# Bias tables in fewer operations, turned keys in a bank of their own, due times moved: one attention and two expert layers on one core

## Chip, core and metric

One core of a Trainium2 chip runs the whole program once per execution. The metric is the device time of one execution in microseconds, the median of several runs. TensorE (PE) multiplies matrices and turns (transposes) tiles, VectorE (DVE), ScalarE (ACT) and GpSimd (POOL) work element by element, SyncE (SP) issues transfers.

## Reference

Three layers follow each other on two sequences of 768 tokens: windowed attention with 8 heads of 64, a gated expert layer, and an expert layer with a layer norm.

```python
scores = scale * q @ k.T                       # per head, 768 x 768
keep = (j < n_global) | ((i - j >= 0) & (i - j < n_local))      # n_global 8, n_local 96
dist = where(j < n_global and not local, n_local, abs(i - j))
scores = where(keep, scores - slope[h] * dist, -1e9)
a = softmax(scores);  x = a @ v
xk, xr = mu_k * x + (1 - mu_k) * x_prev, mu_r * x + (1 - mu_r) * x_prev
x = sigmoid(xr @ w_r) * (relu(xk @ w_k) ** 2 @ w_v)             # 512 -> 1024 -> 512
x = x + relu(layernorm(x) * g_ln @ w_ch1) @ w_ch2               # 512 -> 2048 -> 512
```

All arrays arrive as 8-byte numbers or 4-byte floats. The large weights are 8-byte and are put together into 4-byte words on the chip.

## The kernel before

**Attention.** The 1536 tokens are 12 blocks of 128 (6 for each sequence). A block `n` is done in two half-blocks `i = 2n` and `2n + 1` of four heads each, 24 in all, counted from 0. Block 0 and block 6 see 128 columns, the others 232 (the band and the global columns). For each block its queries and keys are loaded (`plan_loads`, L402 for queries, L353, L354, L356 for keys; L356 and L353 also carry the values), turned on TensorE (L443, in `plan_turn`), and copied to SBUF: queries by VectorE, which scales them (L450), keys by ScalarE (L343 into `b0h`). A half-block then goes through these steps: scores on TensorE (L496); bias added and minimum taken by VectorE (L509, once per head); exponent on ScalarE (L515, once per head); turning of the weights on TensorE into the PSUM tile `b45` (L546, four or eight instructions); one copy `yy<-b` of that tile to SBUF on ScalarE (L343); and the product with the values on TensorE (L561, written x8 in the order and x16 in the profile for a full half-block). There is one tile `b45`, so the weights of half-block `i + 1` can be turned only when the copy of half-block `i` is done. After a block, the inverse sums are spread out, turned on TensorE (L598 in `plan_out`) and multiplied in.

**PSUM banks.** Bank 3 takes the turned queries, the turned keys of all blocks but block 0, and the turned sums (L598). Bank 7 takes the turned keys of block 0, the warm-up products (L248), fillers (L527: products of the identity, of no use to the result, twelve pairs behind the scores of half-blocks 0 to 3), and later the products of the gate.

**Bias tables.** `constants()` makes the table `nb0` (128 x 128, for blocks 0 and 6) and `nb` (128 x 456, for all others) on VectorE from index ramps by GpSimd: L277 to L285 make `nb0`, L288 to L296 make `nb`. The two counts `n_global` and `n_local` arrive in the tile `words` by a transfer of ScalarE's queue (L61). `nb0` is written out before any planned operation, `nb` in four steps that the planner places.

**Weights and expert layers.** Each 512 x 128 piece of 8-byte weights is loaded into `stage` and put together by VectorE in three operations (L628, L629, L630) and split in two parts by ScalarE and GpSimd. The mix of neighbouring tokens (L699 on GpSimd, L704 on VectorE), the gate's products (L755), the hidden layer (L791), the output (L828 to L830), the norms (L871 turns them), and the last layer (L1089 up, L1190 to L1192 down) follow. The gate's products and the first hidden products may run between half-blocks of attention.

**What sets the order.** Every operation is registered with engine costs, the cells that it reads and writes, the buffers ("rooms") that it needs, and a due time. `Plan.play` then simulates a clock for each engine and writes the instructions out in the order in which it picks them: always the one with the smallest pair of earliest start and due time. So a due time decides only between operations that could start at the same moment, and each engine runs its instructions in the order written. `CLOCK` gives the times at which the engines are taken to be free first.

```python
key = (t, due, i, e)
if best is None or key < best:
```

SyncE issues transfers in order too, and a transfer that waits for a buffer holds up those behind it.

## Time and profile before

| | |
|---|---|
| median of 3 runs | 538.32 us (538.18 to 539.33) |
| the profiled execution's own time | 538.67 us |
| its span, first to last instruction | 536.9 us |
| granted TensorE clock | 0.999 of full speed |
| TensorE busy | 525.2 us (98%) |
| VectorE, ScalarE, GpSimd busy | 409.3, 297.7, 284.3 us |

The profiled execution took 1.8 us more than its span and 0.35 us more than the median. A busy share is the time in which an engine had an instruction in work. In the timeline a bracket behind a row is the time for which the engine sat idle before it, with the engine and line that ended it.

### The profile page before, as it was taken

To read this page: it belongs to the slowest core of one execution; us is meant where nothing else is said; L and a number is where in the kernel's file an instruction comes from. 1 tells how busy PE (TensorE), PEld (TensorE's weight loads), DVE (VectorE), ACT (ScalarE), POOL (GpSimd) and SP (SyncE) were. 2 spreads that over 40 slices of the span, in tenths; PEclk is the share of its full clock that TensorE was granted. 3 is DMA by queue.
4 is the path that set the end of the run, shared out by engine and by line. 5 is a ranking of instruction groups with operands and counts; after the bars stand their busy time and mean duration, and the time that the engine had idled before them with its cause. 6 is when DMAs were issued, how large, how long until landed. Compare 5 with 4: busy or idle time off the path is not lost.

```text
span 536.9 us, 8949 instructions
## 1 busy us (share of the span) xinstructions
PE 525.2 (98%) x3231; PEld 457.5 (85%) x3231; DVE 409.3 (76%) x819; ACT 297.7 (55%) x656; POOL 284.3 (53%) x348
## 2 busy tenths in 40 slices
PE   8989999999999999999999999999999999999996
PEld 6867677888899898989888898989888898989885
DVE  5789887973996537558999777687799887778554
ACT  3788979877453235374677453653555446365320
POOL 2387656774855022152249463784785758478300
PEclk9999999999999999999999999999999999999999
DMA  8994584320320000021122003113130321311024
GB/s 161 261 215 99 142 209 121 99 80 2 117 80 2 0 2 1 0 80 40 39 80 78 1 0 117 41 49 109 40 114 5 91 67 43 116 40 39 1 79 159
DMA packets 52110, 40.52 MB, mean 75 GB/s; under 512 B 40928, under 2 KB 41184, under 8 KB 52064
## 3 DMA queue, kind: packets, MB, share of 16 engines
q1 hardware_dynamic: 51200, 39.01, 26.3%
q10 hardware_dynamic: 864, 0.92, 0.5%
q8 instruction: 26, 0.43, 0.3%
q14 instruction: 20, 0.16, 0.1%
HBM read 36.77 MB, written 3.15 MB: 74 GB/s over the span
## 4 chain that ended last, share of the span: by engine, by line
PE 83%; DVE 11%; ACT 2%; DMA 1%; issue 1%; POOL 1%; ACTq 0%; DVEq 0%; SPq 0%
PE b L1089 20%; PE b L791 11%; PE b L1190 8%; PE b L1192 8%; PE b L1191 8%; PE b L755 6%; PE b L496 4%; PE b L561 4%; PE b L546 3%; PE b L828 3%; PE b L830 3%; PE b L829 3%; PE b L443 1%; PE b L527 1%; DVE stage L629 1%
## 5 line engine op out<-in xcount | busy, mean ns | idle before, releaser
L629 DVE SCALAR_TENSOR_TENSOR stage<-stage 128x512 int32<-128x512 int32 x50 | 49.1, 981 | 1.0
L630 DVE SCALAR_TENSOR_TENSOR cv<-cv,stage 128x512 int32<-128x512 int32 x50 | 44.6, 893 | 5.5 <-ACT cv L343 3.8
L515 ACT ACTIVATE t0l<-t0l,mn 128x232 f32<-128x232 f32 (+1 forms) x96 | 44.4, 466 | 6.9 <-DVE mn L509 6.8
L699 POOL TENSOR_SCALAR rt<-xg,vec 128x256 f32<-128x256 f32 x48 | 32.2, 685 | 17.6 <-DVE yy L806 8.8
L1206 DVE TENSOR_TENSOR xg<-b,xg 128x512 f32<-128x512 f32 (+1 forms) x51 | 33.9, 674 | 7.6 <-PE b L1192 6.3
L1108 POOL TENSOR_TENSOR h<-e,h 128x384 fp32r<-128x384 f32 x14 | 17.4, 1243 | 42.2 <-ACT h L343 41.8
L1108 POOL TENSOR_TENSOR h<-rt,h 128x384 fp32r<-128x384 f32 x28 | 37.3, 1331 | 1.7 <-ACT h L343 1.6
L1104 ACT ACTIVATE e<-e 128x384 f32<-128x384 f32 x16 | 8.4, 525 | 47.0 <-DVE e L1097 46.6
L509 DVE CUSTOM_DVE_ANT_0 t0l<-b,ln 128x232 f32<-128x232 f32 x80 | 27.6, 393 | 7.6 <-PE b L496 7.6
L640 POOL TENSOR_TENSOR s<-cv,s 128x384 fp32r<-128x384 f32 (+1 forms) x22 | 25.3, 1154 | 15.0 <-ACT s L636 14.9
L791 PE MATMUL b<-b0l,t1l 128*128 128x256 f32 x144 | 31.7, 281 | 0.0
L628 DVE TENSOR_SCALAR stage<-stage 128x512 int32<-128x512 int32 x50 | 31.0, 619 | 0.8 <-DMA stage<-in_moe_w_ch_dram 0.4
L1196 DVE TENSOR_TENSOR xg<-b,xg 128x1024 f32<-128x1024 f32 x23 | 28.0, 1217 | 4.6 <-PE b L1192 4.2
L704 DVE SCALAR_TENSOR_TENSOR rt<-xg,vec,rt 128x256 f32<-128x256 f32 x48 | 29.6, 662 | 0.6 <-POOL rt L699 0.6
L546 PE MATMUL b<-ident,t0l 128*128 128x128 f32 x176 | 28.8, 282 | 0.1
L1089 PE MATMUL b<-t0h,s 128*128 128x384 f32 x128 | 27.9, 339 | 0.0
L561 PE MATMUL b<-yy,h 128*64 128x128 f32 x352 | 24.5, 279 | 3.3 <-ACT yy L343 3.2
L1089 PE MATMUL b<-t1h,s 128*128 128x384 f32 x128 | 27.6, 337 | 0.0
L866 POOL TENSOR_SCALAR st<-st 128x1 f32<-128x1 f32 x12 | 3.1, 255 | 46.1 <-DVE st L863 45.8
L1033 ACT ACTIVATE cv<-cv,vec 128x256 f32<-128x256 f32 x32 | 14.5, 502 | 23.2 <-DVE cv L630 23.2
L343 ACT ACTIVATE yy<-b 128x1024 f32<-128x1024 f32 (+1 forms) x24 | 22.7, 945 | 7.7 <-PE b L546 7.5
L755 PE MATMUL b<-s,h 128*128 128x512 f32 x96 | 25.8, 404 | 0.0
(316 smaller groups left out, 1708.7 us busy)
## 6 DMA issues: line engine op xcount, KB each, us to landing
stage<-in_moe_w_ch_dram SPq DMA_DIRECT2D x26, 512.0 KB, 3.8
stage<-in_moe_w_k_dram SPq DMA_DIRECT2D x8, 512.0 KB, 4.8
stage<-in_moe_w_v_dram SPq DMA_DIRECT2D x8, 512.0 KB, 3.6
stage<-in_moe_w_ch_dram SPq DMA_DIRECT2D x12, 256.0 KB, 3.0
b0l<-in_q_dram SPq DMA_DIRECT2D x7, 256.0 KB, 3.3
h<-in_v_dram SPq DMA_DIRECT2D x6, 256.0 KB, 5.5
h<-in_v_dram SPq DMA_DIRECT2D x6, 192.0 KB, 4.0
stage<-in_moe_w_r_dram SPq DMA_DIRECT2D x2, 512.0 KB
```

Source lines behind the costliest of these rows:

```text
L515: nc.scalar.activation(t, t, AF.Exp, bias=mn.tile[:, k : k + 1], scale=-1.0, accum_out=sm.tile[:, h : h + 1])
L546: nc.tensor.transpose(b.tile[:, c, k * P : (k + 1) * P], tp.tile[:, o : o + P], self.ident)
L561: nc.tensor.matmul(o, V[c].tile[:, h * D : (h + 1) * D], y.tile[:, c, k * P : (k + 1) * P], start=c == 0, stop=c == m - 1)
L629: p.op({"DVE": 760}, lambda e: nc.vector.scalar_tensor_tensor(low(), high(), -(1 << 31), low(), ALU.bitwise_and, ALU.bitwise_or), [R, (R, ...
L630: p.op({"DVE": 760}, lambda e: nc.vector.scalar_tensor_tensor(y(), y(), 3, low(), ALU.logical_shift_left, ALU.bitwise_or), [(R, 2)], [C], ...
L755: nc.tensor.matmul(b.tile, *seq[s], start=s == 0, stop=s == 11)
L791: nc.tensor.matmul(o, l, r, start=s == 0, stop=s == 11)
L1089: nc.tensor.matmul(acc(x), lhs(i, c, n), rhs(r, j, c), start=y == 0, stop=y == 5)
L1108: lambda e: (nc.vector if e == "DVE" else nc.gpsimd).tensor_tensor(o(1), V(y), o(0).bitcast(F32), ALU.subtract),
L1190: nc.tensor.matmul(ps, hi, wh, start=f == 0, stop=False)
L1191: nc.tensor.matmul(ps, hi, wl, start=False, stop=False)
L1192: nc.tensor.matmul(ps, lo, wh, start=False, stop=f == 1)
```

## The change

1. The bias tables are made with maximum instead of masks: both tables in 13 VectorE operations in place of 15. `nb0` is now planned too, in two steps that wait for `words` (taken to arrive at 5.4 us) and are due 0.6 us after the first block's own due time.
2. The turned keys of blocks 0 to 5 go to bank 7; those of blocks 6 to 11 stay in bank 3.
3. The planner's first free times change (`CLOCK`: TensorE 5.2 to 5.5, VectorE 6.2 to 2.8), transfers start its clock at 2.4 us, and sizes of loads are counted smaller (keys, queries and values by 15%, weights by 37%).
4. Due times of some 20 kinds of operation move, from a fraction of a microsecond to 47 us.

```diff
-CLOCK = {"PE": 5.2, "ACT": 3.0, "DVE": 6.2, "POOL": 4.0, "SP": 0.8}
+CLOCK = {"PE": 5.5, "ACT": 3.0, "DVE": 2.8, "POOL": 4.0, "SP": 0.8, "WORDS": 0.0}
...
-        nc.vector.tensor_scalar(M[:, o], R[:, o], 0.0, None, ALU.is_ge)
+        nc.vector.tensor_scalar(M[:, o], R[:, o], 0.0, BIG, ALU.is_lt, ALU.mult)
+        nc.vector.tensor_tensor(R[:, o], R[:, o], M[:, o], ALU.max)
+        yield
         nc.vector.tensor_copy(f, self.words[:, :, 0])
-        nc.vector.tensor_scalar(G0, J, ng, None, ALU.is_lt)
-        nc.vector.scalar_tensor_tensor(L[:, o], R[:, o], nl, M[:, o], ALU.is_lt, ALU.mult)
-        nc.vector.tensor_tensor(M0, G0, L[:, o], ALU.max)
-        nc.vector.scalar_tensor_tensor(D0, R[:, o], nl, L[:, o], ALU.subtract, ALU.mult)
-        nc.vector.tensor_scalar(M0, M0, -BIG, BIG, ALU.mult, ALU.add)
-        nc.vector.tensor_scalar(D0, D0, nl, None, ALU.add)
-        nc.vector.tensor_tensor(self.nb0, D0, M0, ALU.add)
+        nc.vector.tensor_scalar(M[:, o], R[:, o], nl, BIG, ALU.is_ge, ALU.mult)
+        nc.vector.tensor_scalar(J, J, ng, BIG, ALU.is_ge, ALU.mult)
+        yield
+        nc.vector.tensor_tensor(nb[:, o], R[:, o], M[:, o], ALU.max)
+        nc.vector.scalar_tensor_tensor(self.nb0, J, nl, nb[:, o], ALU.add, ALU.min)
         yield
...
-            p.op({"SP": 60}, lambda e, h=h: nc.sync.dma_start(by_head(qr())[:, h], q[:, h]), (), self.sides(n, s, "q", n % 3), qrooms, due, size=size)
+            p.op({"SP": 60}, lambda e, h=h: nc.sync.dma_start(by_head(qr())[:, h], q[:, h]), (), self.sides(n, s, "q", n % 3), qrooms, due - 20, size=size)
...
-                b = self.bank_room(7 if n == 0 and x == "k" else 3)
+                b = self.bank_room(7 if n < 6 and x == "k" else 3)
...
-        p.op({"PE": 436}, turn, [("x", n)], [("R", n)], [X, b], due + 1)
+        p.op({"PE": 436}, turn, [("x", n)], [("R", n)], [X, b], due + 11)
...
-            p.op({"POOL": 1200}, first, xs + [("vec", 3)], [Y], [X, y] + rooms, due, behind=behind)
+            p.op({"POOL": 1200}, first, xs + [("vec", 3)], [Y], [X, y] + rooms, due - 10, behind=behind)
...
+            p.op({"WORDS": 5400}, lambda e: None, (), ["words"])
+            rooms = [self.token("rt", 2) for _ in range(2)]
+            for ns in (700, 600):
+                p.op({"DVE": ns}, lambda e: next(bias), ["words"], [("nb", False)], [*rooms, self.VW, self.bias], self.due(0) + 0.6)
```

On TensorE, ScalarE, GpSimd and SyncE the same work stands in another order, but for a few small copies and two conversions that go to another engine. The three places of which the rest speaks follow.

VectorE at the start of the program. Before; `words` holds the counts, `rt`, `h1` and `e` the tables in the making, L450 copies the first turned queries out of bank 3:

```order
L277 TENSOR_SCALAR rt_6_92<-rt_5_91 128x128
L278 CAST low_4_90<-words_65 128x2
L279 TENSOR_SCALAR h1_1_74<-h1_1_74,low_4_90 128x128
L280 SCALAR_TENSOR_TENSOR e_7_93<-rt_5_91,low_4_90,rt_6_92 128x128
L281 TENSOR_TENSOR h1_1_74<-h1_1_74,e_7_93 128x128
L282 SCALAR_TENSOR_TENSOR h1_1_74<-rt_5_91,low_4_90,e_7_93 128x128
L283 TENSOR_SCALAR h1_1_74<-h1_1_74 128x128
L284 TENSOR_SCALAR h1_1_74<-h1_1_74,low_4_90 128x128
L285 TENSOR_TENSOR h1_1_74<-h1_1_74 128x128
L450 TENSOR_TENSOR b0l_12_123<-b3_19_156,qs_9_111 128x256
```

And now:

```order
L277 TENSOR_SCALAR rt_6_92<-rt_5_91 128x128
L278 TENSOR_TENSOR rt_5_91<-rt_5_91,rt_6_92 128x128
L583 MEMSET xg_15_134 128x4
L583 MEMSET xg_16_136 128x4
L280 CAST low_4_90<-words_65 128x2
L281 TENSOR_SCALAR rt_6_92<-rt_5_91,low_4_90 128x128
L282 TENSOR_SCALAR h1_1_74<-h1_1_74,low_4_90 128x128
L450 TENSOR_TENSOR b0l_11_115<-b3_20_155,qs_8_103 128x256
L284 TENSOR_TENSOR ln_7_100<-rt_5_91,rt_6_92 128x128
L285 SCALAR_TENSOR_TENSOR h1_1_74<-h1_1_74,low_4_90,ln_7_100 128x128
L450 TENSOR_TENSOR b0l_11_115<-b3_21_161,qs_8_103 128x256
```

The first copy of queries stood behind all nine operations of `nb0`; now two of its operations and the second copy stand behind it.

SyncE's first transfers, before: queries go to `b0l` (those of block 2 to `b0h`), keys to `u`, and the shape 128x4x64 is half of block 0:

```order
L402 DMA b0l_12_123<-in_q_dram 128x4x64
L356 DMA u_13_125<-in_k_dram 128x4x64
L402 DMA b0l_12_123<-in_q_dram 128x4x64
L356 DMA u_13_125<-in_k_dram 128x4x64
L402 DMA b0l_12_123<-in_q_dram 128x8x64
L353 DMA u_13_125<-in_k_dram 96x8x64
L354 DMA u_13_125<-in_k_dram 32x8x64
```

And now:

```order
L402 DMA b0l_11_115<-in_q_dram 128x4x64 x2
L402 DMA b0l_11_115<-in_q_dram 128x8x64
L356 DMA u_12_119<-in_k_dram 128x4x64 x2
L402 DMA b0h_13_122<-in_q_dram 128x8x64
L353 DMA u_12_119<-in_k_dram 96x8x64
L354 DMA u_12_119<-in_k_dram 32x8x64
```

All queries of blocks 0 and 1 are now issued ahead of the first keys, and those of block 2 ahead of the keys of block 1.

TensorE around half-block 4 (the first half of block 2), whose weights are turned into `b45_77` in both programs. Before, from the values' product of half-block 3 on:

```order
L561 MATMUL b6_65_371<-yy_39_239,h1_1_74 64x128 x8
L546 MATMUL b45_77_445<-ident_60,t0l_18_153 128x128 x8
L561 MATMUL b6_82_472<-yy_39_239,h1_1_74 64x128 x8
L443 MATMUL b3_84_489<-ident_60,u_13_125 128x128 x4
L546 MATMUL b45_85_496<-ident_60,t0l_18_153 128x128 x8
L443 MATMUL b3_86_509<-ident_60,b0l_12_123 128x128 x4
L561 MATMUL b6_82_472<-yy_39_239,h1_1_74 64x128 x8
```

And now, from the same product on to the one of half-block 4:

```order
L561 MATMUL b6_70_400<-yy_39_256,h1_1_74 64x128 x8
L443 MATMUL b7_76_449<-ident_60,u_12_119 128x128 x4
L546 MATMUL b45_77_458<-ident_60,t0l_19_149 128x128 x8
L598 MATMUL b3_79_472<-ident_60,xg_15_134 128x128 x4
L496 MATMUL b0_80_479<-b0h_13_122,b0l_11_115 128x232
L496 MATMUL b1_81_480<-b0h_13_122,b0l_11_115 128x232
L496 MATMUL b0_80_479<-b0h_13_122,b0l_11_115 128x232
L496 MATMUL b1_81_480<-b0h_13_122,b0l_11_115 128x232
L443 MATMUL b3_82_488<-ident_60,b0l_11_115 128x128 x4
L443 MATMUL b7_84_495<-ident_60,u_12_119 128x128 x4
L561 MATMUL b6_87_507<-yy_39_256,h1_1_74 64x128 x8
```

Before, the product of half-block 4 (second L561) stands directly behind the turning of its weights; now the turning of sums, the scores of half-block 6 and two turnings of block 4 stand between them.

## Rows read from the trace of the kernel before

**Rows 1.** The page, part 1: TensorE's busy time and share of the span.
```profile
PE 525.2 (98%) x3231; PEld 457.5 (85%) x3231; DVE 409.3 (76%) x819; ACT 297.7 (55%) x656; POOL 284.3 (53%) x348
```

**Rows 2.** Waits of TensorE: engine line <- releaser: us in total, times, longest.
```profile
PE b L561 <- ACT yy L343: 3.2, 4, 1.2
PE b L1190 <- DVE xg L1196: 0.7, 1, 0.7
PE b L871 <- ACT ln L876: 0.6, 1, 0.6
PE b L598 <- DVE b0l L450: 0.4, 1, 0.4
```

**Rows 3.** Timeline of TensorE, 28 to 66 us; idle time before a row in brackets.
```profile
32.12 1.09 PE L561 MATMUL b<-yy,h 128*64 128x128 f32 x16 [1.17 <-ACT yy L343]
33.64 1.04 PE L546 MATMUL b<-ident,t0l 128*128 128x128 f32 x8
35.96 1.09 PE L561 MATMUL b<-yy,h 128*64 128x128 f32 x16 [0.77 <-ACT yy L343]
55.52 1.09 PE L561 MATMUL b<-yy,h 128*64 128x128 f32 x16 [0.41 <-ACT yy L343]
64.25 1.09 PE L561 MATMUL b<-yy,h 128*64 128x128 f32 x16 [0.82 <-ACT yy L343]
```

**Rows 4.** The chain that ended last, 27 to 43 us: start, us, what.
```profile
27.03 0.44 PE b L598 x4
27.46 0.98 PE b L496 x8
28.45 1.02 PE b L561 x16
41.36 1.39 PE b L755 x6
```

**Rows 5.** Timeline of ScalarE, 62 to 65 us: start, us, engine, line, what.
```profile
63.14 1.01 ACT L343 ACTIVATE yy<-b 128x1024 f32<-128x1024 f32 x1
64.04 0.60 ACT L343 ACTIVATE b0h<-b 128x512 f32<-128x512 f32 x1
64.52 0.49 ACT L515 ACTIVATE t0l<-t0l,mn 128x232 f32<-128x232 f32 x1
```

**Rows 6.** Windows, 43.00 to 59.96 us: length, then busy time of each engine.
```profile
43.00:59.96 16.96, 16.55 (x140) 12.57 (x138) 14.13 (x43) 14.90 (x41) 11.51 (x14) 1.00 0.50 125
```

**Rows 7.** Timeline of the first 8 us, VectorE, TensorE and the DMA queue.
```profile
0.84 0.43 SPq L402 DMA_DIRECT2D b0l<-in_q_dram  x1
2.96 0.50 SPq L402 DMA_DIRECT2D b0l<-in_q_dram  x1
5.29 0.17 DVE L278 CAST low<-words 128x2 f32<-128x2 int32 x1 [3.13 <-DMA words<-in_n_local_dram]
5.53 0.63 PE L443 MATMUL b<-ident,b0l 128*128 128x128 f32 x2
7.17 0.41 PE L443 MATMUL b<-ident,u 128*128 128x128 f32 x2 [0.51 <-ACT b0h L343]
7.28 0.42 DVE L450 TENSOR_TENSOR b0l<-b,qs 128x256 f32<-128x256 f32 x1
7.62 0.38 ACT L343 ACTIVATE b0h<-b 128x256 f32<-128x256 f32 x1 [0.29 <-PE b L443]
7.75 0.72 PE L496 MATMUL b<-b0h,b0l 64*128 64x128 f32 x8 [0.16 <-DVE b0l L450]
```

**Rows 8.** DMA issues at 0.84 and 2.96 us: KB, us to landing.
```profile
b0l<-in_q_dram SPq DMA_DIRECT2D x1, 128.0 KB, 3.1
b0l<-in_q_dram SPq DMA_DIRECT2D x1, 256.0 KB, 5.4
```

**Rows 9.** VectorE's rows on `stage`, 40 to 140 us: ns min/median/max.
```profile
L629 DVE SCALAR_TENSOR_TENSOR stage<-stage x14: 675/692/1655, 44.0 to 139.2; 128x512 int32<-128x512 int32 x14
```

**Rows 10.** Groups by line, 0 to 140 us: mean ns of one.
```profile
L704 DVE SCALAR_TENSOR_TENSOR rt<-xg,vec,rt 128x256 f32<-128x256 f32 x23 | 15.1, 696 | 0.0
```

More of the change, by code (lines that the diff above doesn't have):

```diff
@@ L256, in constants @@
         ng, nl = f[:, 0:1], f[:, 1:2]
-        y = [self.t([P, 512], x, bufs=2) for x in ("rt", "rt", "e")]
         C = 2 * WW - MAXG
-        R, M, L = (z[:, 0:C] for z in y)
-        self.nb0, J, G0 = (self.vw[:, 5 * 512 + i * P : 5 * 512 + (i + 1) * P] for i in range(3))
-        D0, M0 = J, G0
+        R, M = (self.t([P, 512], "rt", bufs=2)[:, 0:C] for _ in range(2))
+        self.nb0, J = (self.vw[:, 5 * 512 + i * P : 5 * 512 + (i + 1) * P] for i in range(2))
         iota = lambda x, pattern, base, m: nc.gpsimd.iota(
@@ L413, in plan_values @@
         due = self.due(2 * n) - 4
-        p.op({"SP": 60}, lambda e: self.att_rows(by_head(y.tile), v[t0 : t0 + P], n), (), [("v", n % 4)], [y], due, size=P * DM * 4)
+        p.op({"SP": 60}, lambda e: self.att_rows(by_head(y.tile), v[t0 : t0 + P], n), (), [("v", n % 4)], [y], due, size=P * DM * 3.4)
         g = lambda: self.VW.tile[:, 2048:2560]
@@ L584, in plan_out @@
             else:
-                p.op({"DVE": 170, "ACT": 300}, lambda e: self.copy(e, X.tile[:, :, 0:1], self.X[g - 1].tile[:, :, GT : GT + 1]), [("x", n - 1)], [("x0", g)], [X, self.X[g - 1]], due)
+                p.op({"DVE": 170, "ACT": 300}, lambda e: self.copy(e, X.tile[:, :, 0:1], self.X[g - 1].tile[:, :, GT : GT + 1]), [("x", n - 1)], [("x0", g)], [X, self.X[g - 1]], due + 6)
         sums = [("sm", n, h) for h in range(H)]
@@ L793, in plan_k @@
                     {"PE": 1440}, products, [("xk", g, s, i) for s in range(2) for i in range(2)] + [("m1", c + 4 * (f // 4)) for c in range(4)],
-                    [("kp", g, fp)], rooms + [b] + sorted({self.Wr[c + 4 * (f // 4)][0] for c in range(4)}, key=lambda x: x.tag), due + 3 * fp + 1.5 * u,
+                    [("kp", g, fp)], rooms + [b] + sorted({self.Wr[c + 4 * (f // 4)][0] for c in range(4)}, key=lambda x: x.tag), due + 3 * fp + 1.5 * u + 1.5,
                 )
@@ L835, in plan_v @@
                 [b[tb], *dict.fromkeys(self.k2[g][f // 2][0] for f in fs), *dict.fromkeys(self.Wr[12 + f][0] for f in fs)],
-                due + (3 * n if last else f0), behind=[self.last_pv],
+                due + (3 * n if last else f0) - 1.5, behind=[self.last_pv],
             )
@@ L884, in plan_norm @@
             else:
-                p.op({"ACT": 590}, lambda e: self.copy(e, hi(), chunks(b.tile)), [N], [("B", s, i, 0)], [b, X[0]], due + 3)
-            p.op({"DVE": 715} if early else {"POOL": 1440}, lambda e: sub(e, lo(), chunks(F()), hi().bitcast(F32)), [("F", j), ("B", s, i, 0)], [("B", s, i, 1)], [prep, *X[0:2]], low_due, behind=up)
+                p.op({"ACT": 590}, lambda e: self.copy(e, hi(), chunks(b.tile)), [N], [("B", s, i, 0)], [b, X[0]], due + 14.5)
+            p.op({"DVE": 715} if early else {"POOL": 1440}, lambda e: sub(e, lo(), chunks(F()), hi().bitcast(F32)), [("F", j), ("B", s, i, 0)], [("B", s, i, 1)], [prep, *X[0:2]], low_due + 21.5, behind=up)
             return
@@ L892, in plan_norm @@
         Tt = [("Tt", k) for k in range(4)]
[L893 to L895 removed]
+        p.op({"ACT": 590}, lambda e: self.copy(e, y.tile, b.tile), [], [N], [b, y], due + 3.7)
+        p.op({"DVE": 350}, lambda e: sub(e, T(0), y.tile[:, 0:256], F()[:, 0:256]), [N, ("F", j)], [Tt[0]], [y, prep], due - 16.2)
+        p.op({"DVE": 350}, lambda e: sub(e, T(1), y.tile[:, 256:512], T(0)), [N, Tt[0]], [Tt[1]], [y, prep], due)
         if late:
@@ L899, in plan_norm @@
             p.op({"ACT": 400}, lambda e: self.copy(e, keep(), y.tile[:, 256:512]), [N], [K], [y, prep], due + 3)
-            p.op({"ACT": 400}, lambda e: self.copy(e, hi(), pair(keep())), [K], [("B", s, i, 0)], [prep, X[2]], low_due, behind=[self.x_op])
+            p.op({"ACT": 400}, lambda e: self.copy(e, hi(), pair(keep())), [K], [("B", s, i, 0)], [prep, X[2]], low_due - 20, behind=[self.x_op])
             p.op({"POOL": 700}, lambda e: sub(e, lo(), pair(keep()), hi().bitcast(F32)), [K, ("B", s, i, 0)], [("B", s, i, 1)], [prep, *X[2:4]], low_due)
@@ L1108, in put @@
                 lambda e: (nc.vector if e == "DVE" else nc.gpsimd).tensor_tensor(o(1), V(y), o(0).bitcast(F32), ALU.subtract),
-                [("v", k, y), (*U, 0)], [(*U, 1)], [v[y], h], due + order[x] + 2,
+                [("v", k, y), (*U, 0)], [(*U, 1)], [v[y], h], due + order[x] - 18,
             )
         product("P1", 0, 0)
-        p.op({"ACT": 500}, lambda e: self.copy(e, V(11), acc("P1")), [("up", k, "P1")], [("v", k, 11)], [v[11], banks["P1"]], due + order["P1"] + 1)
+        p.op({"ACT": 500}, lambda e: self.copy(e, V(11), acc("P1")), [("up", k, "P1")], [("v", k, 11)], [v[11], banks["P1"]], due + order['P1'] + 47)
         product("P6", 4, 4)
@@ L1192, in go @@
                         nc.tensor.matmul(ps, lo, wh, start=False, stop=f == 1)
-                    p.op({"PE": 690 if c == whole else 360}, go, [("h", k, f, T, z) for z in range(2)] + [("w2", 2 * q + 1 - f)], [A], [h, rooms[i], chunks[f][0]], d + (0.1 if k else 1.5) * nth + 0.01 * f)
+                    p.op({"PE": 690 if c == whole else 360}, go, [("h", k, f, T, z) for z in range(2)] + [("w2", 2 * q + 1 - f)], [A], [h, rooms[i], chunks[f][0]], d + (0.1 if k else 1.5) * nth + 0.01 * f + 3)
                 cells.append(A)
```

62 lines of the change are left out of this document (30 added, 32 removed).

## Prediction

> **What bounds the kernel now.** Read first the busy shares: TensorE works in 98% of the span [rows 1]. The work on TensorE is the same in both programs, only its order differs, so a faster VectorE or a shorter table is worth nothing in itself: the time changes by what TensorE's idle time changes. The second view is therefore TensorE's own waits [rows 2]. After the first turned queries they come to about 5.6 us in all, and they are the whole stake: 3.2 us in four waits of the values' product (L561) for ScalarE's copy `yy` of the turned weights, 0.4 us of the turned sums (L598) for a copy out of bank 3, 1.3 us in two waits at the passage to the last layer (L871, L1190), and 0.7 us before the first scores [rows 7]. The timeline then shows where the four stand: 1.17 us at 32.12, 0.77 at 35.96, 0.41 at 55.52 and 0.82 at 64.25 [rows 3], which are half-blocks 4, 5, 8 and 10. These four and the one of L598 are all that attention has after its start [rows 2].
>
> Why there? Half-block 4 shows it in the order: the product stands directly behind the turning of its own weights. ScalarE needs 1.01 us for the copy [rows 5], TensorE has nothing in between, and it waits 1.17 us. In half-blocks 5 and 10 one turning of 0.44 us lies between, in 8 some 1.8 us did and still did not do, because ScalarE reached the copy late.
>
> **The start, and the tables.** Before, VectorE begins the nine operations of `nb0` when the counts are there (5.29 us) and takes the first turned queries out of bank 3 at 7.28, though they were turned by 6.16 (5.53 + 0.63) [rows 7]. In the new order only the cast and two operations stand ahead, done by about 6.2, so this copy starts about 1.1 us earlier. This does not make the first scores 1.1 us earlier, because they also need turned keys, and the keys are now the fourth transfer instead of the second. A transfer of 128 KB issued first, at 0.84, landed after 3.1 us, at 3.94; the fifth, with which 768 KB had been asked for, was issued at 2.96 and landed after 5.4, at 8.36 [rows 7, 8]. Between these two points lie 4.42 us for 640 KB. The first keys now complete 640 KB, so I estimate them at 3.94 + 512/640 x 4.42 = 7.5 us; before they completed 256 KB, 4.8 us, and nothing waited for them. The queries of block 2, which now have to be turned before the second scores, complete 1024 KB: 10.1 us. The keys of block 1, which the queries of block 2 now pass too, complete 1280 KB, 11.9 us; they are turned behind second scores, three fillers and the first weights, so after 12 us in any case.
>
> Walked through: second half of queries turned from 6.7 (0.5 idle before) to 7.1; 0.4 idle until the keys; keys turned to 7.9; the queries of block 1 turned while ScalarE copies the keys (0.38) [rows 7]; scores at about 8.4, where they were at 7.75; then the second keys, turned by 9.6, and 0.5 idle for the queries of block 2, behind which the second scores and all else on TensorE stand. That is 1.4 us idle against 0.7: **+0.7 us**. Later the early turnings need not be done again, so a later first score alone costs nothing. Bounds: if no transfer is late, only the first 0.5 is left (-0.2); if the first keys land where the fifth transfer did, at 8.4, +1.6.
>
> The rule that speaks against this edit is in the Trainium skill, "DMA: Bandwidth & Descriptors", section on queues, rings and completion order: each engine consumes a queue's descriptors in ring order, so queries put ahead of keys are served ahead of them. The two landings agree as far as they go. By the fabric ceiling of 435 GB/s among that page's specifications, the 384 KB put in front would cost an estimated 0.9 us, the keys would land at about 5.7, and the start would come out at -0.2 + 0.5 = +0.3 us; the rows show a slower queue.
>
> The six operations of the larger table are as many as before and lie between first scores and their use three half-blocks later, behind fillers: nothing. The shorter `nb0` by itself: nothing beyond the above.
>
> **Attention between 30 and 70 us.** The new order puts half-block i + 2's scores between the turning of half-block i and its product, everywhere from half-block 4 on. One such piece is scores of 0.98 and one turning of 0.44 to 0.48, so at least 1.4 us of cover where there was none or 0.44; half-block 4 has four pieces, 0.44 + 0.98 + 2 x 0.44 = 2.3 us [rows 4]. Waits plus cover were 1.17, 1.21 and 1.26 us for half-blocks 4, 5 and 10, so 1.4 us covers all three.
>
> Can ScalarE keep this pace? In half-blocks 5 to 9 a cycle of TensorE is one product (1.02), one turning of weights (1.04), scores (0.98) and one small turning (0.44): 3.48 us [rows 3, 4]. ScalarE has four exponents, the copy and one or two copies of a turned tile. From start to start the copy takes 0.90 and a small one 0.48 [rows 5]; with exponents at 0.48, the stretch between two copies, in which three exponents and two small copies stand, is 0.90 + 0.96 + 1.44 = 3.3 us. So it fits with 0.18 to spare, and a late exponent will still be felt now and then. I leave two waits of the size seen at half-block 8, 0.41 each: 0.8, and 0.1 for the rest. The 0.4 at L598 was a wait for queries' copy out of bank 3; with the keys gone from that bank it has two users for each block instead of three, and I count this wait as gone. **3.55 - 0.9 = -2.65 us.** Bounds: no wait left (-3.55); a wait of 0.41 in each of seven half-blocks (-0.7).
>
> **What moves without price.** The gate's products, moved out of half-blocks 6 to 9 to behind half-block 12, are done by TensorE in any case; they were cover there, and later they still are. If attention ends 2 us earlier, the next that could be late are the hidden layer's weight pieces, for which TensorE waits nowhere now; (b) below prices that. The operations moved in the hidden and last layers stand where TensorE does not idle, except the passage with 1.3 us. I change nothing there: between 0 and -1.3 if the new order also removes these. The tail behind the last product is the same, row for row.
>
> **Sum.** Own time 538.67 + 0.7 - 2.65 = 536.7 us; the median of the runs lies 0.35 below, so **536.4 us**.
>
> **Rivals.** (a) *ScalarE sets the pace.* In the stretch 43.00 to 59.96, with one wait, it was busy 14.90 of 16.96 us, 88% [rows 6]. If it cannot be kept busier, 3.3 us of work take 3.75, TensorE waits 0.27 us in each of nine half-blocks, 2.4 us, and the gain is 1.1 instead of 2.65: 538.32 + 0.7 - 1.1 = 537.9. Against it: 88% is what the old order asked for in a stretch with only one wait; nothing shows that it is a ceiling.
>
> (b) *VectorE becomes the bound near half-block 19.* Weight pieces held back early meet later: between the minima of half-blocks 18 and 19 the new order has two L628, five L629 and L630, four L704 and three more of their width. TensorE has meanwhile four halves of the gate's products (1.39 each), two halves of a product, 1.04 of turning and some 1.6 of small turnings: 10.2 us [rows 3, 4]. At 0.69 for a two-input row and for L628, L704 and the three alike, VectorE needs 9.7 us and is in time. But L629 has been seen at 1.66 [rows 9, 10]; if all five take that, it is 14.6, 4.4 late, of which I take 0.9 as covered by the products between half-block 19's scores and its turning: 536.4 + 3.5 = 539.9, slower. It decides once VectorE is 3.9 us late there (3.0 past the cover); against it speaks the median of 0.69.
>
> (c) *The queries in front cost nothing* because transfers overlap more than the two landings let me see, and half-blocks 4 to 12 lose every wait: 538.32 - 0.2 - 3.55 = 534.6.
>
> **Chances.** Forecast 0.47 (of it 0.05 ends within 0.2%), (a) 0.25, (b) 0.13, (c) 0.15. Within 0.2%, about 1.1 us, a measurement of this kernel hardly tells a change from none. So faster 0.42 + 0.15 = 0.57, same 0.05 + 0.25 = 0.30, slower 0.13. For the range I leave out half of (b) and the far end of (c): 534.4 to 539.2. The forecast's own range, by the bounds of its two terms, is 534.6 to 539.2: 538.32 - 3.75 and 538.32 + 0.9.
>
> **What would show it.** Right: the first L450 near 6.2 us; first scores later than 7.75 with TensorE waiting for a transfer of keys; no wait over 0.5 us at half-blocks 4, 5, 10; L598 not waiting. Wrong: L561 or L546 waiting at many half-blocks for L343 or L515 by about 0.3 each (a); L546 of half-block 19 waiting behind L509, with L629 and L630 well over 1 us (b); new waits in the last layer, whose order was also changed and of which I assume nothing.

## Result, and the profile after

The changed kernel takes **541.86 us** (median of 5 runs, 541.39 to 542.01) against 538.73 before (5 runs, 538.18 to 539.33): ratio 1.0056, 95% interval 1.0045 to 1.0066. It is slower by 3.1 us; forecast was 536.4 us, and the range ended at 539.2.

The page of the changed kernel, part 1, answers to [rows 1], and TensorE's waits behind the warm-up to [rows 2] (engine line <- releaser: us in total, times, longest; one more, of 0.2 us, is left out):

```profile
PE 527.2 (98%) x3231; PEld 458.7 (85%) x3231; DVE 413.0 (76%) x813; ACT 296.5 (55%) x656; POOL 279.1 (52%) x352
```
```profile
PE b L496 <- ACT b0h L343: 1.9, 2, 1.1
PE b L871 <- ACT rt L876: 1.2, 1, 1.2
PE b L496 <- DVE mn L509: 1.0, 1, 1.0
PE b L828 <- DVE xg L842: 0.7, 2, 0.5
PE b L443 <- DVE b0l L450: 0.6, 1, 0.6
PE b L527 <- ACT b0h L343: 0.6, 1, 0.6
PE b L791 <- DVE rt L801: 0.5, 1, 0.5
PE b L1193 <- DVE xg L1199: 0.4, 1, 0.4
PE b L443 <- DMA u<-in_k_dram: 0.2, 1, 0.2
```

The waits of L561 for ScalarE's copy and of L598 are gone, as forecast. Scores (L496) wait instead, for keys' copies and for minima, and at the passage to the last layer more rows wait than before.

**Where the time went.** Both programs give TensorE the same instructions, so they can be laid side by side by work done. I gave each instruction the mean step (start to next start) of its shape from the kernel before, taken where TensorE did not idle, 523.5 us in all, and noted when each kernel's TensorE stood at a given amount of it. Other ways of forming the mean move the differences by up to 0.2 us:

```
work done (us)              24     64    120    240    300    520
before, at (us)           30.1   76.2  132.6  250.5  311.5  529.2
changed, against before   +1.3   -2.3   +1.0   +1.6   +3.3   +3.5
gained (-) or lost (+)    +1.3   -3.6   +3.3   +0.6   +1.8   +0.2
```

The start costs 1.3, the early half-blocks give back 3.6: at 64 us of work, where half-block 14 is under way, the change is 2.3 us ahead. It loses 3.3 in the rest of attention, 0.6 in the hidden layer, which I did not follow, and 1.8 at the passage to the last layer. The tail gives back 0.3, which leaves the 3.2 us between the two spans.

What is different in the middle is VectorE. Windows of the kernel before, then of the changed one (length, then busy time and rows of PE, PEld, DVE, ACT, POOL, then clock, DMA share, GB/s):

```profile
56.00:110.00 54.00, 52.59 (x472) 41.73 (x470) 45.81 (x142) 48.58 (x138) 34.98 (x42) 1.00 0.56 142
```
```profile
56.00:110.00 54.00, 50.82 (x428) 41.60 (x428) 53.50 (x138) 45.46 (x126) 40.58 (x45) 1.00 0.49 133
```

VectorE goes from 45.8 to 53.5 us of 54, with four rows fewer. The mixes (L704) alone grew by as much, 7.7 us; these are their windows, before and changed (only L704's own VectorE time stands here, with the count):

```profile
56.00:110.00 54.00, 3.05 (x6) 1.00 0.56 142
```
```profile
56.00:110.00 54.00, 10.72 (x12) 1.00 0.49 133
```

Twice as many mixes stand there, since the fifth to the twelfth now start between 62.8 and 79.4 us and not between 43.2 and 65.2, and a mix there takes 0.89 us on the mean in place of 0.51. Timeline of the changed kernel around the wait of half-block 20's scores, 95 to 103 us:

```profile
95.69 2.44 POOL L699 TENSOR_SCALAR rt<-xg,vec 128x256 f32<-128x256 f32 x4
98.09 1.05 POOL L425 COPY h<-h 32x512 f32<-32x512 f32 x1
98.59 3.27 DVE L704 SCALAR_TENSOR_TENSOR rt<-xg,vec,rt 128x256 f32<-128x256 f32 x4
99.11 1.28 POOL L640 TENSOR_TENSOR s<-cv,s 128x512 fp32r<-128x512 f32 x1
101.10 0.63 ACT L707 ACTIVATE h<-rt 128x512 fp32r<-128x512 f32 x1 [1.76 <-DVE rt L704]
101.64 0.58 ACT L343 ACTIVATE b0h<-b 128x512 f32<-128x512 f32 x1
102.39 1.21 PE L496 MATMUL b<-b0h,b0l 64*128 64x232 f32 x8 [1.13 <-ACT b0h L343]
```

TensorE is said to wait for ScalarE's copy of keys, but that copy stands in ScalarE's queue behind L707, which waited 1.76 us for the mixes. So it was VectorE that was late, two queues away. The scores of half-block 13 waited 0.97 us for minima (L509) behind an L628 of 1.47 us, ahead of the first moved mix, and those of 18 waited 0.74 us for a copy of keys whose ScalarE had waited for minima.

### The profile page after: what moved, and what is told of

Read it like the earlier page. It is cut to its first block, busy times and chain, and to the rows that moved or that the text cites. A ratio compares the mean times of both kernels' runs of the same rounds, so it can differ in the third digit from the quotient of the medians.

```text
span 540.1 us, 8939 instructions
## 1 busy us (share of the span) xinstructions
PE 527.2 (98%) x3231; PEld 458.7 (85%) x3231; DVE 413.0 (76%) x813; ACT 296.5 (55%) x656; POOL 279.1 (52%) x352
## 4 chain that ended last, share of the span: by engine, by line
PE 81%; DVE 15%; ACT 1%; DMA 1%; issue 1%; POOL 1%; SPq 0%; DVEq 0%; ACTq 0%
PE b L1092 20%; PE b L791 11%; PE b L1194 8%; PE b L1193 8%; PE b L1195 8%; PE b L755 5%; PE b L828 3%; PE b L830 3%; PE b L829 3%; PE b L496 3%; PE b L561 3%; PE b L546 2%; DVE t0l L509 2%; DVE stage L629 2%; DVE cv L630 2%; DVE rt L704 2%
## 5 line engine op out<-in xcount | busy, mean ns | idle before, releaser
L629 DVE SCALAR_TENSOR_TENSOR stage<-stage 128x512 int32<-128x512 int32 x50 | 51.6, 1033 | 0.7
L699 POOL TENSOR_SCALAR rt<-xg,vec 128x256 f32<-128x256 f32 x48 | 31.7, 672 | 28.3 <-DVE u L806 9.4
L630 DVE SCALAR_TENSOR_TENSOR cv<-cv,stage 128x512 int32<-128x512 int32 x50 | 42.7, 856 | 0.4
L628 DVE TENSOR_SCALAR stage<-stage 128x512 int32<-128x512 int32 x50 | 35.4, 709 | 6.1 <-DMA stage<-in_moe_w_ch_dram 4.9
L1111 POOL TENSOR_TENSOR h<-rt,h 128x384 fp32r<-128x384 f32 x28 | 34.5, 1234 | 5.3 <-ACT h L343 5.1
L640 POOL TENSOR_TENSOR s<-cv,s 128x384 fp32r<-128x384 f32 (+1 forms) x22 | 25.2, 1149 | 16.3 <-ACT s L636 16.0
L1111 POOL TENSOR_TENSOR h<-e,h 128x384 fp32r<-128x384 f32 x14 | 17.0, 1214 | 31.7 <-ACT h L343 31.6
L791 PE MATMUL b<-b0l,t1l 128*128 128x256 f32 x144 | 32.3, 282 | 0.0
L704 DVE SCALAR_TENSOR_TENSOR rt<-xg,vec,rt 128x256 f32<-128x256 f32 x48 | 31.3, 701 | 0.6 <-POOL rt L699 0.6
L509 DVE CUSTOM_DVE_ANT_0 t0l<-b,ln 128x232 f32<-128x232 f32 x80 | 27.8, 387 | 3.0 <-PE b L496 2.9
L496 PE MATMUL b<-b0h,b0l 64*128 64x232 f32 (+1 forms) x192 | 25.2, 369 | 3.0 <-ACT b0h L343 1.9
L343 ACT ACTIVATE cv<-stage 128x512 f32<-128x512 f32 x35 | 23.4, 668 | 7.0 <-DMA stage<-in_moe_w_ch_dram 3.7
L546 PE MATMUL b<-ident,t0l 128*128 128x128 f32 x176 | 26.8, 277 | 0.2 <-ACT t0l L515 0.2
L801 DVE SCALAR_TENSOR_TENSOR rt<-b,rt 128x512 f32<-128x512 f32 x24 | 16.3, 684 | 13.8 <-ACT rt L800 13.7
```

The source lines that it names most:

```text
L496: nc.tensor.matmul(S(k), self.qT(n)[r, c], self.kT()[r, c, c0:c1], start=True, stop=True)
L629: p.op({"DVE": 760}, lambda e: nc.vector.scalar_tensor_tensor(low(), high(), -(1 << 31), low(), ALU.bitwise_and, ALU.bitwise_or), [R, (R, ...
L630: p.op({"DVE": 760}, lambda e: nc.vector.scalar_tensor_tensor(y(), y(), 3, low(), ALU.logical_shift_left, ALU.bitwise_or), [(R, 2)], [C], ...
L704: nc.vector.scalar_tensor_tensor(y.tile[:, u], z, v, y.tile[:, u], ALU.mult, ALU.add)
L791: nc.tensor.matmul(o, l, r, start=s == 0, stop=s == 11)
L1111: lambda e: (nc.vector if e == "DVE" else nc.gpsimd).tensor_tensor(o(1), V(y), o(0).bitcast(F32), ALU.subtract),
```

## Experiments

All kernels are compared with the kernel before in the same group of runs (538.5 to 538.9 us there). The expectations say "half-block 9" and "12" for the start of the loss; counted in the order, the waiting scores are those of half-blocks 13, 18 and 20.

**VectorE relieved, order kept.** The second of VectorE's three operations on a weight piece (L629) is left out, in the changed kernel (e2) and in the one before (e3):

```diff
-        p.op({"DVE": 760}, lambda e: nc.vector.scalar_tensor_tensor(low(), high(), -(1 << 31), low(), ALU.bitwise_and, ALU.bitwise_or), [R, (R, 1)], [(R, 2)], [raw], due - 1.7)
+        p.op({"DVE": 760}, lambda e: None, [R, (R, 1)], [(R, 2)], [raw], due - 1.7)
```

In e5 VectorE's half of the mix (L704) is left out of the changed kernel:

```diff
-            p.op({"DVE": 1400}, second, xs + [("vec", m)], [Y], [X, y], due)
+            p.op({"DVE": 1400}, lambda e: None, xs + [("vec", m)], [Y], [X, y], due)
```

> The changed kernel without the second of the three operations that put a weight piece together (the 50 rows of L629, 51.6 us of VectorE); the order on TensorE stays the same, the weights come out wrong. Theory A (VectorE is what TensorE waits for from 56 to 110 us and between 235 and 300): both losses go, 541.9 - 3.3 - 2.4 = 536.2 us, and the wait of scores for L509 at 58 us and the two for the keys' copy at 87 and 102 us are gone. Rival C (the new order itself makes TensorE wait, by its place of scores and by late transfers of keys): at most 1 us is gained, 541 us or more, and the three waits stay.

> The kernel before without the same second operation of each weight piece; the order on TensorE stays the same, the weights come out wrong. Theory A (before, attention waited for ScalarE's copy and VectorE had slack, 85% busy from 56 to 110 us): little is gained, 537.5 to 538.5 us, with the waits of L561 for the copy still there; then the new order without this operation (536.2 expected) is faster than the old one without it. Rival C: 537.5 to 538.5 as well, but the new order without it stays at 541 or more.

> The changed kernel without VectorE's half of the mix of neighbouring tokens (all 48 rows of L704, 31.3 us of VectorE, of which 12 rows with 10.7 us lie between 56 and 110 us, where the kernel before had 6 rows with 3.05); the order on TensorE stays the same, the gate gets only the other half. Theory A (the mixes moved behind half-block 12, each of them slowed, are what VectorE is late for): the waits at 87 and 102 us go and some 2.5 to 3 us are regained, 539 us, more than the 2.5 that leaving out L629 gave with 50 us of work. Rival C (the weight pieces L628 to L630 alone hold VectorE up): under 1 us, 541 us or more.

Without L629 the changed kernel took 539.36 us (ratio 1.0007, interval 0.9992 to 1.0023) and the kernel before 537.69 (0.9977, 0.9964 to 0.9989). A gain of 2.5 against 1.0: theory A had the direction and 3 us too much, and the new order stayed the slower one. The wait of half-block 18 went, that of 13 stayed, and that of half-block 20 grew from 1.13 to 2.19 us, since the row that held it up had grown (in the second line ns min/median/max):

```profile
95.77 6.08 DVE L704 SCALAR_TENSOR_TENSOR rt<-xg,vec,rt 128x256 f32<-128x256 f32 x4
```
```profile
L704 DVE SCALAR_TENSOR_TENSOR rt<-xg,vec,rt x4: 472/652/4533, 95.8 to 101.4; 128x256 f32<-128x256 f32 x4
```

Four mixes took 6.08 us, and one of them 4.53; alone one takes 0.47. Less work on VectorE had moved them into a stretch in which GpSimd worked without a break. Without the mixes the changed kernel took 538.68 us (1.0001, 0.9990 to 1.0012), as theory A expected, and was ahead of the kernel before by 1.9 us at 120 us of work, where the full one is 1.0 behind. The wait of half-block 20 went. Those of half-blocks 13 (0.95) and 18 (0.68) stayed, although A had named the second. So the mixes at their new place account for the longest wait, not for all three. The kernel before was not run without its mixes.

**GpSimd's reads taken away, order kept.** GpSimd subtracts the high from the full weights (L640, two inputs in SBUF, 64 rows). Here it fills the low half with zero, which writes as much and reads nothing. A fill is also shorter: the 64 rows take 31.1 us of GpSimd in place of 82.9.

```diff
-            (nc.vector if e == "DVE" else nc.gpsimd).tensor_tensor(lo, x(), hi.bitcast(F32), ALU.subtract)
+            if e == "DVE":
+                nc.vector.tensor_tensor(lo, x(), hi.bitcast(F32), ALU.subtract)
+            else:
+                nc.gpsimd.memset(lo.bitcast(F32), 0.0)
```

> The changed kernel with GpSimd's low halves of the weight pieces (the 22 and more rows of L640 on GpSimd, 1.1 to 1.3 us each) replaced by a fill with zero, which reads no SBUF; the order stays the same, the weights lose their low half. VectorE's own work is untouched. Theory A (VectorE is late because its rows of two inputs take 1.4 to 1.7 us in place of 0.7 while GpSimd works): VectorE's busy time falls by 10 us or more, L629 falls from a mean of 1.03 to about 0.85 us, and 1.5 to 3 us are regained, 539 to 540.5. Rival E (VectorE has simply more rows there, whatever GpSimd does): its rows keep their length and the time stays at 541.9, within 0.5.

> The kernel before with GpSimd's low halves of the weight pieces (L640 on GpSimd) replaced by a fill with zero; the order stays the same, the weights lose their low half. The control for the run that did this to the changed kernel and gained 6.7 us. Theory A (GpSimd's reads slow VectorE in both kernels, but only the new order has VectorE on the path behind half-block 9): 537.5 to 538.5 us, since the waits for ScalarE's copy `yy` stay, and the new order is then the faster by 2 us or more. Rival F (the fill speeds up both kernels alike): 532 to 533 us.

The changed kernel took **535.12 us** (0.9937, 0.9921 to 0.9952), the kernel before 537.03 (0.9971, 0.9961 to 0.9981), 0.5 below what was expected of it. VectorE had the same instructions; L629, first with GpSimd's reads (changed kernel), then with fills (ns min/median/max):

```profile
L629 DVE SCALAR_TENSOR_TENSOR stage<-stage x50: 674/846/1675, 15.3 to 494.6; 128x512 int32<-128x512 int32 x50
```
```profile
L629 DVE SCALAR_TENSOR_TENSOR stage<-stage x50: 642/693/1484, 15.3 to 486.9; 128x512 int32<-128x512 int32 x50
```

The window of the middle with fills, to compare with the one above:

```profile
56.00:110.00 54.00, 53.69 (x453) 44.47 (x454) 47.43 (x141) 47.32 (x134) 33.95 (x49) 1.00 0.50 133
```

VectorE falls from 53.5 to 47.4, and no scores wait any more; at 300 us of work the kernel is 4.1 us ahead of the one before. Theory A holds, and was sized too small (539 to 540.5). Subtractions in place of fills cost the order before 1.8 us and the new order 6.7.

Is it the reads, or only that GpSimd works longer? Single rows tell. In e6 and e9 together, 16 rows of L629, L630 and L704 lay beside fills and no other row of GpSimd. They took 0.68 to 0.69 us (L704 0.47), as with GpSimd idle. One of them in e9, and then an L628 of e6 beside two fills:

```profile
361.83 0.52 POOL L643 MEMSET w<- 128x512 f32 x1
362.12 0.68 DVE L630 SCALAR_TENSOR_TENSOR cv<-cv,stage 128x512 int32<-128x512 int32 x1
```
```profile
473.03 0.88 POOL L643 MEMSET s<- 128x384 f32 x2
473.10 1.09 DVE L628 TENSOR_SCALAR stage<-stage 128x512 int32<-128x512 int32 x1
```

L628 takes 0.42 us alone, so it was slowed by fills too. It has one input, but it is the row that held up half-block 13. How much of the 6.7 us comes from the fills' shorter time is not shown.

With fills in both, the new order is the faster one by 1.9 us, which is the number that was forecast (2.65 less 0.7). That the number fits is in part luck. Its parts, e6 against e9, are +1.2 at the start, -3.6 to 64 us of work, -0.9 from there to 240, +0.8 at the passage and +0.8 behind it.

**The same work on VectorE.** Nothing is left out: VectorE makes those low halves itself.

```diff
-            (nc.vector if e == "DVE" else nc.gpsimd).tensor_tensor(lo, x(), hi.bitcast(F32), ALU.subtract)
+            nc.vector.tensor_tensor(lo, x(), hi.bitcast(F32), ALU.subtract)
```

> The changed kernel with all low halves of weight pieces that GpSimd made (L640, 64 rows of 1.15 to 1.4 us) made by VectorE at the same places of the order; nothing is left out. VectorE gets 64 rows of 0.57 to 0.69 us, some 40 us over the program and 6 us between 56 and 110 us, and loses the slowing by L640, which the run with fills put at some 24 us over the program and 6 us in that stretch. Theory A: the two cancel about there, elsewhere VectorE has slack: 540 to 543 us. Rival O (the slowing was worth more than the rows): 537 us or less, faster than both kernels.

> The kernel before with the low halves of weight pieces on VectorE, nothing left out. Theory A (before, VectorE had slack and the waits for ScalarE's copy were the loss): 537.5 to 538.7 us, as with the fills, of which the run gave 537.0. Rival Q (64 rows more on VectorE at places made for GpSimd put new waits into the old order): 539 us or more.

The changed kernel took 538.64 us (1.0005, 0.9994 to 1.0016), 3.2 less than with the halves on GpSimd; the kernel before 539.34 (1.0015, 1.0006 to 1.0024), 0.85 more. Theory A's 540 to 543 was too dear for the first, but rival O's 537 did not come either; for the second A's 537.5 to 538.7 was too cheap and rival Q came true: in the old order the new rows cost more than the slowing did. So 64 more rows on VectorE, with GpSimd relieved of them, make the new order faster: what they take away was worth more there. Laid side by side by work done, it gains 1.4 us up to 120 us, 0.7 from there to 240 and 1.5 at the passage; the waits of half-blocks 13, 18 and 20 stay, with 0.8, 1.4 and 0.8 us. It only draws level with the kernel before.

**The passage to the last layer.** In e7 the kernel before gets the new due times of the norms and the last layer (all edits of the change from L873 on but the tables' own); in e8 the changed kernel gets the old ones back. In e14 it gets back those of the hidden layer and the output (L794 to L843), in e1 both sets. One line of each set, as in e7 and e14:

```diff
-                [("acc", k, m, i)], [("x1", g, tb), cell], [rooms[i]], d + 2.8,
+                [("acc", k, m, i)], [("x1", g, tb), cell], [rooms[i]], d + 8.8,
```
```diff
-                [("vp", g, tb), ("e", g, tb)], [("x1", g, tb)], [b[tb], y, x1], due + 10.5,
+                [("vp", g, tb), ("e", g, tb)], [("x1", g, tb)], [b[tb], y, x1], due + 9,
```

> The kernel before with the new due times of the norms and the last layer alone; attention, the gate and the hidden layer keep their order on TensorE up to the first turned norm. Theory A (the new due times of norms and last layer lose time between 235 and 300 us by themselves): about +1.5 to +2.4 us, 540.3 to 541. Rival B (that loss is handed on by the attention's and gate's new order): 538.7 us, within 0.5.

> The changed kernel with the old due times of the norms and the last layer, attention and the gate in the order of the changed kernel (the earlier run with these and the hidden layer's due times set back had moved attention as well). Theory A: 1.5 to 2.4 us are regained, 539.5 to 540.4 us. Rival B: 541.9 us, within 0.5.

> The changed kernel with the hidden layer's and the output's due times set back, norms and last layer as in the change. Two runs have shown that the old norm and last-layer times cost 2.2 us in the changed kernel and the new ones 4.1 us in the old. Theory K (these sets of due times are fitted to each other): slower than 541.9 by 1 us or more, the loss lying between 240 and 300 us. Rival L (the hidden layer's new times are what loses there): 539.5 to 540.5 us.

> The changed kernel, with the due times of the hidden layer, the output, the norms and the last layer set back to those before; the order of attention is the same as in the changed kernel up to its end. Measured: 541.9 us for the change, 538.7 before. Theory A (attention's second half loses 3.3 us because VectorE is full from 56 to 110 us, and the new due times of the later layers lose another 2.4 us between 235 and 300 us): the second loss goes, 539.5 us. Rival B (the later loss is what the late attention hands on: VectorE's weight work that was put off): 541.9 us, no change. In both, TensorE's waits up to 130 us stay.

All four were slower: 542.80 (e7, 1.0074, 1.0061 to 1.0087), 544.08 (e8), 546.34 (e14) and 546.28 us (e1). The new late times cost the old kernel 4.1 us, all between 240 and 300 us of work, and spare the new one 2.2. In e7 theory A had the direction and half the size. In e8 and e1 neither A nor B held, and in e14 theory K had the sign, but its loss lies between 90 and 100 us of work (last section), as e1's does, and not between 240 and 300. It looks as if these times were fitted to the order ahead of them; no run shows why. One wait could be followed. In the changed kernel (GpSimd's part of the last norm, then VectorE, ScalarE, TensorE):

```profile
287.80 0.55 POOL L867 TENSOR_TENSOR st<-st,mhalf 128x1 f32<-128x1 f32 x1
291.69 1.10 DVE L1111 TENSOR_TENSOR h<-e,h 128x384 fp32r<-128x384 f32 x1
293.05 0.22 DVE L875 SCALAR_TENSOR_TENSOR st<-st 128x1 f32<-128x1 f32 x2
293.23 0.82 ACT L876 ACTIVATE rt<-xg,st 128x512 f32<-128x512 f32 x1 [0.21 <-DVE st L875]
294.10 0.65 PE L871 MATMUL b<-ident,rt 128*128 128x128 f32 x4 [1.18 <-ACT rt L876]
```

L875 takes 0.15 us and could have run from 288.4; at `due + 21` it stands behind a slowed L1111 and others until 293.05. I set it back to `due + 1`, on top of the halves on VectorE:

```diff
-        p.op({"DVE": 100}, lambda e: nc.vector.scalar_tensor_tensor(st.tile[:, 1:2], st.tile[:, 6:7], -1.0, st.tile[:, 0:1], ALU.mult, ALU.mult), [], [N], [st], due + 21)
+        p.op({"DVE": 100}, lambda e: nc.vector.scalar_tensor_tensor(st.tile[:, 1:2], st.tile[:, 6:7], -1.0, st.tile[:, 0:1], ALU.mult, ALU.mult), [], [N], [st], due + 1)
```

> The changed kernel with the low halves of weight pieces on VectorE and the norms' small operation (L875) due as before. With the splits on VectorE alone (538.64 us) L875 stood behind L630, a slowed L1111 and L628 at 290.1 us, 4.7 us after GpSimd's part of the norm was done, and TensorE waited 1.2 us for L876 behind it. Theory A: L875 comes earlier, the wait goes, 537.4 us, faster than both kernels by about 1. Rival P (as with every other set of due times taken back alone, the new places cost more elsewhere): 538.6 us or more.

It took 539.57 us (1.0025, 1.0016 to 1.0035), 0.9 more than without. The wait of 1.2 for L876 shrank to 0.15, and TensorE waited 0.48, 0.43 and 0.74 at three other places. Rival P came true.

**Other parts undone in the changed kernel.** One part each, everything else as changed: e4 the planner's first times, with `FIRST_BYTES` and the sizes of loads; e10 the tables (15 operations, `nb0` ahead of the plan); e11 the keys' bank; e12 the queries' loads; e13 the due times of L629 and L630; e15 the turned sums. A line of each but e10:

```diff
-CLOCK = {"PE": 5.5, "ACT": 3.0, "DVE": 2.8, "POOL": 4.0, "SP": 0.8, "WORDS": 0.0}
+CLOCK = {"PE": 5.2, "ACT": 3.0, "DVE": 6.2, "POOL": 4.0, "SP": 0.8, "WORDS": 0.0}
...
-                b = self.bank_room(7 if n < 6 and x == "k" else 3)
+                b = self.bank_room(7 if n == 0 and x == "k" else 3)
...
-            p.op({"SP": 60}, lambda e, h=h: nc.sync.dma_start(by_head(qr())[:, h], q[:, h]), (), self.sides(n, s, "q", n % 3), qrooms, due - 20, size=size)
+            p.op({"SP": 60}, lambda e, h=h: nc.sync.dma_start(by_head(qr())[:, h], q[:, h]), (), self.sides(n, s, "q", n % 3), qrooms, due, size=size)
...
-        p.op({"DVE": 760}, lambda e: nc.vector.scalar_tensor_tensor(y(), y(), 3, low(), ALU.logical_shift_left, ALU.bitwise_or), [(R, 2)], [C], [raw, cv], due - 2.5)
+        p.op({"DVE": 760}, lambda e: nc.vector.scalar_tensor_tensor(y(), y(), 3, low(), ALU.logical_shift_left, ALU.bitwise_or), [(R, 2)], [C], [raw, cv], due - 1)
...
-        p.op({"PE": 436}, turn, [("x", n)], [("R", n)], [X, b], due + 11)
+        p.op({"PE": 436}, turn, [("x", n)], [("R", n)], [X, b], due + 1)
```

> The changed kernel with the planner's first free times, the start of the transfers' clock and the sizes of loads as before; then the gate's first four products stand behind half-blocks 11 to 13 in place of 14 and 15, and its first mixed tokens behind half-block 12 in place of 14. Theory A (bunching of conversions and mixes on VectorE behind half-block 12): VectorE is less full from 56 to 110 us, and 1 to 2 us are regained, 540 to 541 us. Rival D (the loss comes from where the due times of attention put the scores, not from when the gate's work comes): 541.9 us or more.

> The changed kernel with the old bias tables: 15 operations in place of 13, `nb0` written ahead of all planned work. Theory A (a shorter table is worth nothing in itself; the loss is made behind half-block 9): the first copy of queries comes 1 us later, the gate's first products move from behind half-blocks 14 and 15 to behind 12 and 13, and the time stays within 1.5 us of 541.9. Rival G (planning the tables is what spoils the order): 538 to 539.5 us.

> The changed kernel with the turned keys of blocks 1 to 5 in bank 3 again. Theory A (the bank frees the early half-blocks of a wait or two but has no part in the loss): the early gain of 2.3 us up to half-block 10 shrinks by 0.4 us for a wait of L598 or of turned keys, the loss behind it stays: 542 to 543 us. Rival H (the keys out of bank 3 let the scores run ahead and so pile the weight pieces up behind half-block 9): 540 us or less.

> The changed kernel with queries and keys loaded in turn as before (the due time of the queries' loads set back by 20 us). Theory A (putting queries in front costs 1.3 us at the start): the keys of block 0 land about 2 us earlier, the first 1.3 us are regained and no more: 540 to 541 us. Rival I (the start's delay is taken up by slack later): 541.9 us, within 0.5.

> The changed kernel with the old due times of the second and third operation of a weight piece (L629, L630). Theory A (where VectorE's slowed two-input work stands decides): the loss between 64 and 120 us changes by more than 1 us, and with it the time, either way; the 2.8 us between 240 and 300 us change too, since the last layer's pieces go through the same lines. Rival J (these due times matter little): 541.9 us, within 1.

> The changed kernel with the turned sums (L598) due as before, 10 us earlier. In the change they come later, and with them the group's output, the mixes (L704) and the gate's products. Theory M (the later sums are what piles the mixes up behind half-block 12): the first twelve mixes come before 62 us, VectorE is below 95% from 56 to 110 us, 538.5 to 540.5 us. Rival N (the mixes are late for another reason, such as the arrival of the gate's weights): 541.9 us or more, VectorE as full.

Measured: e4 546.83, e10 552.58, e11 546.88, e12 546.26, e13 545.39, e15 550.40 us. Every one is slower than the change itself (541.86), by 3.5 to 10.7 us; no expected gain came, and no price for an undone part (A in e10 and e11) was near. In e13 theory A, more than 1 us either way, held. In e10 both tables stood ahead of the first copy of queries, which came at 9.51 us instead of 6.27; the planner was still told that VectorE is free at 2.8. In e12 the first 1.3 us were regained at 12 us of work, as expected, and then 5.4 lost in new waits. In e15 the first twelve mixes began by 79.8 us, as in the change (79.4), and theory M fell, although VectorE was less busy from 56 to 110 us, as M said: 48.8 us of 54, and 47.2 in e4. So VectorE's share of that stretch does not settle the time by itself. What the runs do tell is that no single part, taken back, returns the loss. Which one puts the mixes late is not settled: with the old clock and sizes (e4) the fifth to the twelfth began between 56.2 and 76.1 us, part of the way back.

## Why the prediction was wrong

**The start: right, a size off.** Forecast were the first copy of queries near 6.2, keys at 7.5, scores at 8.4, and +0.7 us. In the changed kernel:

```profile
6.27 0.42 DVE L450 TENSOR_TENSOR b0l<-b,qs 128x256 f32<-128x256 f32 x1 [0.37 <-PE b L443]
7.58 0.44 PE L443 MATMUL b<-ident,u 128*128 128x128 f32 x2 [0.21 <-DMA u<-in_k_dram]
8.54 0.72 PE L496 MATMUL b<-b0h,b0l 64*128 64x128 f32 x8
15.04 0.71 PE L527 MATMUL b<-ident 128*128 128x128 f32 x4 [0.58 <-ACT b0h L343]
```

The cost was 1.25. The wait for block 2's queries did not come; one of 0.58 for a copy of keys at 15.04 did, and single turnings between fillers took longer. The estimate of the keys' landing from the two landings of [rows 7, 8] held; the 5.7 us worked out from the ceiling of the Trainium skill's "DMA: Bandwidth & Descriptors" did not. Of the 6857 packets of the first 12 us, 6759 were under 512 bytes.

**Attention between 30 and 70 us: right, sized 1 us short.** Forecast -2.65, bound -3.55; measured -3.6, although 1.2 us were lost again at half-block 13's scores. A wait cost more than its idle time: the step into half-block 4's product, with 1.17 us of idle [rows 3], was 1.3 longer than the mean step of its shape, and all five waits together cost 4.4 us in place of 3.55. Every wait of [rows 3] is gone, and rival (a), ScalarE's pace, did not show: from 30 to 56 us ScalarE was busy 24.78 of 26 us and TensorE 25.97.

**"What moves without price": wrong, and this is the step that failed.** The gate's products were looked at as work of TensorE alone ("are done by TensorE in any case"). With them went the mixes on VectorE and GpSimd that feed them, into a stretch full of weight pieces. Cost 3.3 us instead of nothing. Rival (b) had the mechanism, VectorE late with slowed rows, and the place of the longest wait. Between the minima of half-blocks 18 and 19 VectorE had the very rows that (b) counted (length of the window, then busy time of PE, PEld, DVE, ACT, POOL):

```profile
89.52:101.78 12.26, 11.74 (x98) 9.74 (x96) 11.92 (x16) 7.74 (x18) 10.59 (x11) 1.00 0.44 136
```

They took 12.2 us where (b) counted 9.7 at the median and 14.6 at the worst. The next minima began 2.8 us behind the end of half-block 19's scores, and TensorE waited 1.13 us, at half-block 20's scores and not at the turning that (b) named. With fills on GpSimd (e6) the same rows took 10.1 us. I believed the median of [rows 9] and gave (b) 0.13; and VectorE was late at half-block 18 too, at 13 inside the stretch counted above, and at 129 us, where L791 waited 0.46 us for L801. [rows 9] had the price: 692 ns at the median, 1655 at most, and GpSimd was at work in the long ones. What I did not ask was what GpSimd does at the new place.

The Trainium skill's "SBUF — State Buffer", section "Who interferes with whom", states that a VectorE instruction with two inputs in SBUF contends with a GpSimd instruction that reads SBUF, not with one that only writes it. The runs agree: fills in place of reads took L629 from a mean of 1.03 to 0.78 us, and the 16 two-input rows beside fills alone were not slowed, while L509, which takes one input from PSUM, kept 387 to 389 ns. L628 has one input and was slowed in both, so the sentence does not cover it.

**The passage: wrong.** "I change nothing there: between 0 and -1.3" was +1.8. The runs tie about half of it to GpSimd's subtractions: with fills in both orders the new one still loses 0.8 there (e6 against e9). One wait of 1.2, at L871, comes from L875's place and stays with fills (1.19). The due times that would mend it were not found, so the cause of the rest is open.

**The sum** up to 64 us of work was -1.95 by forecast and -2.3 measured; it is that close because the start was 0.55 dearer and attention 0.95 cheaper than forecast. All that followed, +5.8 us up to the tail, comes from the steps counted at nothing.

## What to carry to other kernels

An engine at 76% over the whole program can be at 99% in the stretch into which work is moved: price a moved operation at its new place, with all that feeds it on every engine. VectorE's rows with two SBUF inputs had two prices here, 0.69 us with GpSimd idle or filling and up to 1.69 in the changed kernel with GpSimd reading beside them; read the spread of a row and what GpSimd did in the long ones, not the median. Due times that were moved together are one edit: taking any of these parts back cost 2 to 11 us, so this change was understood by taking work away under a fixed order, not by undoing its parts.
